# The two stores of the last product's halves issued from ScalarE's queue

## The chip, the cores and the metric

One core of a Trainium2 chip runs the whole kernel. The metric is the device time of one execution in microseconds (us); the kernel before takes 207.64 us, the median of three runs from 207.38 to 207.97. Its engines are TensorE (PE in the profile: matmuls, with PEld for weight loads), VectorE (DVE), ScalarE (ACT), GpSimd (POOL) and SyncE (SP), which computes nothing and issues transfers. Transfers can be issued from the instruction streams of SP, ACT and POOL; an issue is an instruction of that stream and waits there for what it needs.

## The reference

A decaying linear attention over 4 batches, 8 heads, 768 positions and 64 dimensions feeds a feed-forward layer with a leaky activation:

```python
for b in range(nb):                                    # blocks of 64 positions
    intra = (qb @ kb.T * Dmask) @ vb
    inter = (qb * lam_pow) @ kv_state
    out[block] = intra + inter
    kv_state = lam_block * kv_state + (kb * rev_pow).T @ vb
x = attn_out                                           # [3072, 512]
h = x @ w_in                                           # [3072, 2048]
g = max(h, 0) + alpha * min(h, 0)
return g @ w_out                                       # [3072, 512], float32
```

The change is in the way the last rows of `g @ w_out` are written out.

## The kernel before

The 3072 rows are worked through in six chunks of 512 (`c` from 0 to 5). A chunk holds 256 positions of two batches. For each, the attention part makes `xT` (512 features by 512 rows, fp16), `up` multiplies it by `w_in` and applies the activation, giving `g` in fp16, and a down projection multiplies `g` by `w_out`. The order of the instructions is written out by hand; every engine runs its stream in that order, and waits between engines are semaphores. Chunk `c`'s down projection runs among the up projection of chunk `c + 1`; the last chunk's comes after everything else, in `down2_last`, called in line 1105 as the last thing the kernel does.

The down projection of chunks 3 to 5 goes by seven products in place of eight: the rows of `g` are parted by even and odd positions, its features and the columns of `w_out` by halves, and sums and differences of these parts are multiplied. The products are numbered 1 to 7 and run in the order of `CHAIN` (line 640). Each product has eight matmuls of 128 rows by 256 columns for each batch `b`, in line 655. `evacuated` (line 673) then takes the result from PSUM: for products 1, 5, 6 and 4 ScalarE copies it into an output tile in SBUF (line 687), for 2, 3 and 7 VectorE adds it to such a tile (line 690). Products 2, 3, 4 and 7 each finish a quarter of the chunk's output, and `write` stores it.

In `down2_last` the two batches are taken one after the other, so each store has 128 rows of 256 floats, 128 KB. The last four steps are product 3 of batch 0, product 4 of batch 0, product 3 of batch 1, product 4 of batch 1. The very last one, `(i, b) == (4, 1)`, is cut into two halves of 128 columns (lines 714 to 720). Each half has a PSUM bank of its own ("s" and "acc"), eight matmuls, a VectorE add of 128x128 (line 719) to the tile `c21`, into which ScalarE has copied the sum so far (line 685), and a store of 64 KB by `write` (line 720).

All stores of the down projections are issued by SP, in line 589, 669 or 671. The nine of `down2_last` are those of line 671: seven of 128 KB and the two halves. After the last, SP waits until every transfer has landed (line 1131 in the profile, which is the end of the kernel), and a barrier of all engines closes it.

ScalarE issues one transfer in the kernel before, the load of `lam` in line 62.

Of the kernel before, what the change touches and what calls it, by code (L numbers as in the profile page):

```python
# [11 lines left out]
def kernel(  # L12
# [16 lines left out]
    nc = tc.nc  # L29
# [102 lines left out]
    def bank_of(bank, name, dtype=fp32):  # L132
        pool = h_ps_pool if bank == "h" else ps
        return pool.tile([128, CH], dtype, tag=bank, name=name)
# [25 lines left out]
    for half in range(2):  # L160
# [7 lines left out]
        out=drop, in0=rel_i, scalar1=0.0, scalar2=-1e30, op0=ALU.is_lt, op1=ALU.mult  # L168
# [458 lines left out]
    def g_sum(c, i, j, eng, b=None):  # L627

        a11, a12, a21, a22 = [part_of(c, j, half, e, b) for e in range(2) for half in range(2)]
        s1 = sums[3].rearrange("p f (b j) -> p f b j", b=2)[:, ds(2 * j, 2)]  # L630
        s1 = s1.rearrange("p i b j -> p i (b j)") if b is None else s1[:, :, b]
        out, in0, in1, op = {
            1: (s1, a21, a22, ALU.add),
            3: (a21, a11, a21, ALU.subtract),
            2: (a11, s1, a11, ALU.subtract),
            4: (a12, a12, a11, ALU.subtract),
        }[i]
        engine(eng).tensor_tensor(out=out, in0=in0, in1=in1, op=op)  # L638
# [3 lines left out]
    def product(c, i, b, t, fresh, last, cols, of=ds(0, 256)):  # L642

        for f in range(NF // 2):
            x = sums[3][:, f, ds(b * L, L)] if i == 5 else g_of(c, f + 8 * (i in (2, 3, 4)))[:, int(i in (4, 7)), b]
            w = {
                1: halves[0][0],
                2: halves[1][0],
                3: halves[1][1],
                4: sums[2],  # L650
                5: sums[0],
                6: sums[1],
                7: halves[0][1],
            }[i][:, f, of]
            nc.tensor.matmul(  # L655
                t[:, cols],
                lhsT=x,
                rhs=w,
                start=(fresh and f == 0),
                stop=(last and f == NF // 2 - 1),  # L660
                skip_group_check=True,
            )

    def write(c, e, half, o, b=None, of=ds(0, 256)):
        pb = c // 2
        to = out.rearrange("(x s) d -> x s d", x=B)[ds(2 * (c % 2), 2), ds(pb * W, W), ds(256 * half, 256)]
        to = to.rearrange("x (j e) d -> e j x d", e=2)[e]
        if b is None:
            nc.sync.dma_start(out=to, in_=o)
        else:  # L670
            nc.sync.dma_start(out=to[:, b, of], in_=o)

    def evacuated(c, i, t, b=None):

        X = O.setdefault((c, "out"), {})

        def tile_of(name):
            if name not in X:
                X[name] = o_pool.tile([128, 2, 256], fp32, tag="osb", name="o_sb")
            return X[name] if b is None else X[name][:, b]  # L680

        t = t.rearrange("p (x d) -> p x d", d=256) if b is None else t
        where = {2: ("c11", 0, 0), 3: ("c12", 0, 1), 4: ("c21", 1, 0), 7: ("c22", 1, 1)}
        if i is None:
            nc.scalar.activation(tile_of("c21"), t, AF.Copy)
        elif i in (1, 5, 6, 4):
            nc.scalar.activation(tile_of({1: "c11", 5: "c22", 6: "c12", 4: "c21"}[i]), t, AF.Copy)  # L687
        else:
            o = tile_of(where[i][0])
            nc.vector.tensor_tensor(out=o, in0=o, in1=t, op=ALU.add)  # L690
        if i in where:
            name, e, half = where[i]
            write(c, e, half, tile_of(name), b)
# [12 lines left out]
    def down2_last(c):  # L706

        order = [(i, side, b) for i, side in CHAIN[:5] for b in range(2)]
        order += [(3, 1, 0), (4, 0, 0), (3, 1, 1), (4, 0, 1)]
        for i, side, b in order:  # L710
            if i in (1, 2):
                O[c, side, b] = bank_of({(0, 0): "op", (1, 0): "tk"}.get((side, b), "h"), "o_ps")
            t = O[c, side, b]
            if (i, b) == (4, 1):
                for x, bank in enumerate(("s", "acc")):
                    p4 = ps.tile([128, 2, CH], fp32, tag=bank, name="p4")[:, 0]
                    product(c, i, b, p4, True, True, ds(0, 128), ds(128 * x, 128))
                    o = O[c, "out"]["c21"][:, b, ds(128 * x, 128)]
                    nc.vector.tensor_tensor(out=o, in0=o, in1=p4[:, 0:128], op=ALU.add)
                    write(c, 1, 0, o, b, ds(128 * x, 128))  # L720
                continue
            product(c, i, b, t, i in (1, 2, 5), i in (2, 3, 4), ds(0, 256))
            evacuated(c, i, t[:, 0:256], b)
            if (i, b) == (7, 1):
                evacuated(c, None, t[:, 0:256], b)
            if i == 1:
                for j in range(4):
                    g_sum(c, 2, j, "V", b)
            if i == 2 and b == 1:
                for j in range(4):  # L730
                    g_sum(c, 4, j, "V")
# [350 lines left out]
    for c, at in plan.items():  # L1082
        u = d = w = 0
        for x, what in enumerate(order[c]):
# [18 lines left out]
            if c == 4 and 9 <= x <= 12:  # L1103
                weight_sum(3, x - 9)
    down2_last(NC - 1)


# [28 lines left out]
```

## Time and profile before

| | |
|---|---|
| Median of three runs | 207.64 us (207.38 to 207.97) |
| The profiled execution | 207.89 us |
| Its span, first to last instruction | 206.1 us |
| Mean granted TensorE clock | 0.996 |
| PE busy | 200.1 us, 97% of the span |
| DVE busy | 159.1 us, 77% |
| ACT busy | 113.6 us, 55% |
| POOL busy | 110.3 us, 54% |
| Stores of line 671 | 9, the first issued at 193.9 us, the last at 203.2 us |
| Length of one such issue | shortest 332 ns, median 344 ns, longest 1178 ns |

The span leaves out what the run does around the program's first and last instruction, 1.8 us here. A row of the timeline has the start in us, the length in us, the engine, the line, the operation and the tiles; "SPq" and "ACTq" are the instruction streams of SP and ACT, where issues of transfers are listed and are not counted as busy. A row of the DMA view gives, for a stretch of time, the issues that began in it with their size and the time from issue to landing, that is until the transfer's completion was counted. "x2" at the end of a timeline row means that two neighbouring instructions were merged, with the gap between them in the length.

### The profile page before, as it was taken

What the parts mean: (1) busy time and instruction counts of PE and PEld (TensorE: products, weight loads), DVE (VectorE), ACT (ScalarE), POOL (GpSimd) and SP (SyncE); (2) the same over time, 40 slices, a digit from 0 to 9 for tenths busy, and PEclk for the clock granted to TensorE, in tenths of its full rate; (3) what the DMA queues carried; (4) which work ended last, traced back from release to release, by engine and by line L of the source; (5) the groups of instructions that cost most, each with busy time, mean ns of one, the idle gap of its engine ahead of it and who ended that gap; (6) DMA issues with size and microseconds to landing.
All of it is one profiled execution on the core that took longest, in us unless ns stands there. A gap on an engine that the chain in (4) does not pass through costs nothing.

```text
span 206.1 us, 5587 instructions
## 1 busy us (share of the span) xinstructions
PE 200.1 (97%) x2271; PEld 122.8 (60%) x2271; DVE 159.1 (77%) x289; ACT 113.6 (55%) x210; POOL 110.3 (54%) x132
## 2 busy tenths in 40 slices
PE   7999999999999999999999999999999999999991
PEld 6976445556445465555555455467667666667881
DVE  6978889568889647899998897959999466675921
ACT  7885778144776218656767466643543644444220
POOL 8999794043468893196356995562094040642000
PEclk9999999999999999999999999999999999999998
DMA  6999999997999998999969974441001201012222
GB/s 164 277 197 234 244 260 206 234 287 231 225 230 257 203 237 189 245 158 125 188 108 276 213 176 88 64 102 42 12 0 54 90 15 51 2 54 71 83 77 79
DMA packets 58206, 31.18 MB, mean 151 GB/s; under 512 B 27124, under 2 KB 55940, under 8 KB 58180
## 3 DMA queue, kind: packets, MB, share of 16 engines
q1 hardware_dynamic: 43028, 21.25, 42.5%
q0 software_dynamic: 15136, 9.57, 29.3%
q8 instruction: 18, 0.29, 0.6%
q14 instruction: 8, 0.07, 0.1%
q10 hardware_dynamic: 16, 0.00, 0.0%
HBM read 27.27 MB, written 6.29 MB: 163 GB/s over the span
## 4 chain that ended last, share of the span: by engine, by line
PE 92%; DVE 2%; ACT 2%; issue 1%; ACTq 0%; DVEq 0%
PE h_ps L545 39%; PE o_ps L573 21%; PE o_ps L655 16%; PE s L391 4%; PE acc L416 3%; PE unread L152 3%; PE acc L375 2%; PE tpx L341 2%; PE acc L436 1%; DVE g L638 1%; ACT L180 1%; ACT m L553 1%; ACT xT L250 1%; DVE sm L402 1%; PE p L655 0%
## 5 line engine op out<-in xcount | busy, mean ns | idle before, releaser
L545 PE MATMUL h_ps<-xT,w_in_sb 128*128 128x512 f16 (+1 forms) x392 | 91.9, 375 | 0.2 <-DVE g L560 0.2
L560 DVE SCALAR_TENSOR_TENSOR g<-m,oma,h_ps 128x512 f16<-128x512 f32 (+1 forms) x98 | 71.1, 734 | 24.9 <-ACT m L553 21.7
L553 ACT ACTIVATE m<-h_ps 128x512 f32<-128x512 f32 (+1 forms) x98 | 57.3, 588 | 46.3 <-PE h_ps L545 40.3
L545 PEld LDWEIGHTS <-w_in_sb 128*128 128x128 f16 x392 | 37.6, 98 | 37.4 <-issue 0.4
L573 PE MATMUL o_ps<-w_out_sb,g 128*128 128x512 f16 x192 | 46.8, 380 | 0.0
L402 DVE TENSOR_TENSOR sm<-s,dmask 128x1024 f16<-128x1024 f32 x24 | 29.2, 1219 | 11.7 <-PE s L391 11.7
L655 PEld LDWEIGHTS <-g 128*128 128x128 f16 x296 | 28.2, 98 | 8.2
L638 POOL TENSOR_TENSOR s<-g 128x512 f16<-128x512 f16 x11 | 13.0, 1179 | 32.8 <-PE o_ps L655 16.7
L573 PEld LDWEIGHTS <-g 128*128 128x128 f16 x192 | 17.7, 98 | 19.4 <-DVE g L560 0.2
L250 ACT ACTIVATE xT<-acc 128x512 f16<-128x512 f32 x24 | 14.3, 597 | 24.2 <-PE acc L436 22.2
L355 POOL TENSOR_TENSOR qdT<-qkT,qdecay 128x512 f16<-128x512 f16 (+1 forms) x19 | 20.5, 1082 | 7.6 <-DMA qkT<-qk 4.5
L655 PE MATMUL o_ps<-w_out_sb,g 128*128 128x256 f16 x192 | 24.1, 273 | 0.0
L291 POOL TENSOR_TENSOR kdec<-kraw,kdecay 128x512 f16<-128x512 f32 x18 | 20.0, 1116 | 6.1 <-DMA kraw<-in_k_dram 6.0
L254 POOL CAST qk<-qraw 128x512 f16<-128x512 f32 x12 | 7.6, 637 | 16.7 <-DMA qraw<-in_q_dram 15.9
L465 DVE SCALAR_TENSOR_TENSOR R<-R,rdecay,acc 128x128 f16<-128x128 f16 x54 | 15.5, 340 | 0.0
L278 POOL DMA_DIRECT2D v<-in_v_dram x19 | 14.9, 789 | 0.4 <-issue 0.4
L638 POOL TENSOR_TENSOR g<-g 128x512 f16<-128x512 f16 x11 | 13.3, 1207 | 0.9
L687 ACT ACTIVATE o_sb<-o_ps 128x512 f32<-128x512 f32 (+1 forms) x15 | 7.5, 497 | 7.6 <-PE o_ps L655 7.6
L655 PE MATMUL o_ps<-w_sum,g 128*128 128x256 f16 x88 | 11.3, 273 | 0.0
L391 PE MATMUL s<-qkT 64*64 64x128 f16 x384 | 10.1, 221 | 0.0
L416 PE MATMUL acc<-sm,v 64*64 64x128 f16 x384 | 9.8, 218 | 0.0
L690 DVE TENSOR_TENSOR o_sb<-o_sb,o_ps 128x512 f32<-128x512 f32 (+1 forms) x12 | 6.5, 549 | 4.2 <-PE o_ps L655 2.2
(84 smaller groups left out, 194.2 us busy)
## 6 DMA issues: line engine op xcount, KB each, us to landing
out_dram<-o_sb SPq DMA_DIRECT2D x20, 256.0 KB, 3.0
kraw<-in_k_dram SPq DMA_DIRECT2D x7, 512.0 KB, 5.3
qraw<-in_q_dram SPq DMA_DIRECT2D x6, 512.0 KB, 5.5
v<-in_v_dram POOLq DMA_DIRECT2D x19, 128.0 KB, 5.1
w_in_sb<-in_moe_w_in_dram POOLq DMA_DIRECT2D x4, 512.0 KB, 8.5
w_out_sb<-in_moe_w_out_dram POOLq DMA_DIRECT2D x4, 512.0 KB, 10.5
qraw<-in_q_dram POOLq DMA_DIRECT2D x6, 256.0 KB, 7.1
qraw<-in_q_dram SPq DMA_DIRECT2D x6, 256.0 KB, 4.8
```

Of the source, the lines that this page charges most:

```text
L250: nc.scalar.activation(out, in_, AF.Copy)
L291: engine(eng).tensor_tensor(out=kdec, in0=kr, in1=kdecay[:, ds(4 * hh, 4), :].rearrange("p h e -> p e h").unsqueeze(3).to_broadcast([128, ...
L355: engine(eng).tensor_tensor(out=qdT[:, :, :, p], in0=(t["qps"] if eng == "P" else t["qkT"][:, 0])[:, :, :, p], in1=qdecay[:, hh, :, :, p], ...
L391: nc.tensor.matmul(t["s"][ds(a * 64, 64), hl, hp, 1 - e, :].rearrange("p (e j) -> p e j", e=2), lhsT=t["qkT"][p, 1, e, hp, ds(a * 64, 64)] ...
L402: nc.vector.tensor_tensor(out=t["sm"].rearrange("p a h x j -> p (a h) x j"), in0=t["s"].rearrange("p a h x j -> p (a h) x j"), in1=mask_of ...
L416: nc.tensor.matmul(ot[a][ds(hl * 64, 64), hp, :], lhsT=t["v16"][p, 2 * hp + hl, e, :], rhs=t["sm"][p, hl, hp, 1 - e, :], start=(2 * pb + a ...
L545: nc.tensor.matmul(h_ps[:, 0:n] if bi is None else h_ps[:, 0:n].rearrange("p (e j) -> p e j", e=2), lhsT=w_in_sb[:, gi, ts(f, 128)], rhs=x ...
L553: nc.scalar.activation(m[:, 0:n], h_ps[:, 0:n], AF.Relu, scale=-1.0)
L560: nc.vector.scalar_tensor_tensor(out=g, in0=mv, scalar=oma[:, f : f + 1], in1=hv, op0=ALU.mult, op1=ALU.add)
L573: nc.tensor.matmul(o_ps, lhsT=lhs(c, f, t), rhs=w_out_sb[:, f, :], start=(f == 0), stop=(f == NF - 1),)
L638: engine(eng).tensor_tensor(out=out, in0=in0, in1=in1, op=op)
L655: nc.tensor.matmul(t[:, cols], lhsT=x, rhs=w, start=(fresh and f == 0), stop=(last and f == NF // 2 - 1), skip_group_check=True,)
```

## The change

`write` gets a parameter for the engine whose stream issues the store, with SP as its default, and the call for the two halves of the last product passes ScalarE. All other calls stay on SP.

```diff
-    def write(c, e, half, o, b=None, of=ds(0, 256)):
+    def write(c, e, half, o, b=None, of=ds(0, 256), queue=nc.sync):
...
         if b is None:
             nc.sync.dma_start(out=to, in_=o)
         else:
-            nc.sync.dma_start(out=to[:, b, of], in_=o)
+            queue.dma_start(out=to[:, b, of], in_=o)
...
                     nc.vector.tensor_tensor(out=o, in0=o, in1=p4[:, 0:128], op=ALU.add)
-                    write(c, 1, 0, o, b, ds(128 * x, 128))
+                    write(c, 1, 0, o, b, ds(128 * x, 128), nc.scalar)
```

Two of the nine stores of line 671 are thereby issued from ScalarE's stream, with the same tiles, sizes and places in the output as before.

## The prediction

> **What bounds the kernel now.** I read the page's engine table and its chain of waits first, then the timeline of the last six microseconds, then the DMA view of narrow windows there, and last what SyncE (SP) waits for at the end.
>
> ```profile
> PE 200.1 (97%) x2271; PEld 122.8 (60%) x2271; DVE 159.1 (77%) x289; ACT 113.6 (55%) x210; POOL 110.3 (54%) x132
> PE 92%; DVE 2%; ACT 2%; issue 1%; ACTq 0%; DVEq 0%
> 201.00 0.91 PE p L655 x16
> 201.93 0.29 DVE o_sb L719
> ```
>
> The first two lines are the engines' busy time and the chain's shares, the other two the end of the chain in order of time (start, length, what). Up to 201.9 us TensorE is the bound, and the change touches none of it. But the chain stops at the last VectorE add, at 201.93 + 0.29 = 202.22, and the span is 206.1. What lies in the 3.9 us between is stores, and the change is there and nowhere else.
>
> ```profile
> 200.16 0.38 ACT L687 ACTIVATE o_sb<-o_ps 128x256 f32<-128x256 f32 x1 [0.84 <-PE o_ps L655]
> 201.03 0.42 DVE L690 TENSOR_TENSOR o_sb<-o_sb,o_ps 128x256 f32<-128x256 f32 x1 [1.32 <-PE o_ps L655]
> 201.54 0.68 DVE L719 TENSOR_TENSOR o_sb<-o_sb,p 128x128 f32<-128x128 f32 x2
> 199.74 0.33 SPq L671 DMA_DIRECT2D out_dram<-o_sb  x1
> 200.57 0.33 SPq L671 DMA_DIRECT2D out_dram<-o_sb  x1
> 201.48 1.18 SPq L671 DMA_DIRECT2D out_dram<-o_sb  x1
> 202.75 0.38 SPq L671 DMA_DIRECT2D out_dram<-o_sb  x1
> 203.23 0.41 SPq L671 DMA_DIRECT2D out_dram<-o_sb  x1
> ```
>
> These are timeline rows: start, length, engine. The last five stores start at 199.74, 200.57, 201.48, 202.75 and 203.23; call the last three A, B and C. B and C are the two halves that the change moves. A is the store of the product before, and stays on SP. A's data are ready at 201.03 + 0.42 = 201.45 and it starts 0.03 later, so SP is on time there. But issuing A takes 1.18 us, where the two stores of the same size ahead of it took 0.33. B's data are ready when the first of the two adds at L719 ends; the pair runs from 201.54 to 202.22 and the second starts at 201.93, so the first, as long as the second, ends at 201.83. SP gets to B at 202.75, 0.92 late, and to C at 203.23, 1.01 late. That lateness is what the change can win.
>
> ```profile
> DMA packets 28, 0.04 MB, mean 440 GB/s; under 512 B 0, under 2 KB 27, under 8 KB 27
> q8 instruction: 1, 0.02, 100.9%
> 202.27:202.66 0.39, 0.00 (x0) 0.00 (x0) 0.00 (x0) 0.00 (x0) 0.00 (x0) 1.00 0.08 11
> q8 instruction: 1, 0.02, 57.4%
> 155.56 0.38 SPq L669 DMA_DIRECT2D out_dram<-o_sb  x1
> ```
>
> Why A takes so long: the first two rows are the DMA view of 200.6 to 200.7. One packet in it is not a store's but an instruction fetch, 16 KB in one packet and so on one DMA engine of 16. Its share, 100.9% of 16 engines' 0.1 us, makes 1.61 us, so that engine is taken until about 202.3. The third row is a stretch of the windows view (its last two columns are DMA share and GB/s): from 202.27 to 202.66 only 0.08 of the 16 engines is busy, one engine or little more, which is the late one making up its part of earlier stores. A's issue ends at 202.66, 0.4 after the fetch: an ordinary issue, begun when the late engine came free. The last two rows are a fetch between 155.5 and 155.6 with a single store beside it, which took its usual 0.38. So a fetch alone doesn't hold an issue; it held A, when that engine already owed parts of earlier stores.
>
> ```profile
> out_dram<-o_sb SPq DMA_DIRECT2D x1, 128.0 KB, 2.7
> out_dram<-o_sb SPq DMA_DIRECT2D x1, 64.0 KB, 1.7
> SPq L1131 <- DMA out_dram<-o_sb: 0.5, 2, 0.3
> SPq L1131 <- DMA out_dram<-o_sb: 0.4, 1, 0.4
> L1131 SPq EVENT_SEMAPHORE  x11: 17/28/28, 203.7 to 206.1; - x11
> L1131 SPq DRAIN  x3: 7/7/13, 205.3 to 205.6; - x3
> ```
>
> Landings: A lands 2.7 after its start, at 201.48 + 2.7 = 204.2; B at 202.75 + 1.7 = 204.45; C at 203.23 + 1.7 = 204.94. The waits are SP's at the end of the kernel, in 204 to 204.25 and in 204.55 to 205: it waits for these landings in their order and last for C. From C's landing to the span's end are 206.1 - 204.94 = 1.16 us of closing waits and barriers, which the change leaves alone.
>
> **The change, part by part.** Removed: two issues of 0.38 and 0.41 on SP, the last two that it has. Added: the same two on ScalarE (ACT), each behind the wait for VectorE's add that it had on SP. No byte, add or matmul changes.
>
> Where they land on ACT: its last operation ends at 200.16 + 0.38 = 200.54. Behind the moved issues there is only the closing drain, so nobody is held by a wait there. ACT's idleness is the cover for the 0.8 us of issuing; an ACT busy past 202.7 would take the gain away.
>
> They are moved past one item of SP's queue, A. If ACT can issue while A is held on SP: B starts at 201.83 + 0.03 = 201.86 and takes 0.38, to 202.24. C's data are there at 202.22, and the gap between B and C on SP was 203.23 - 202.75 - 0.38 = 0.10, so C starts at 202.34 and lands at 202.34 + 1.7 = 204.04. That is before A's landing at 204.2. What is late next is A, on SP. So the end moves from 204.94 to 204.2, 0.74 us, and no further.
>
> Two things come off. SP looks at the landings in order and has, after A's, two more waits to pass, where now it has none of these after C. Between C's landing at 204.94 and its drain at 205.3 it passes some five waits, about 0.07 each, an estimate from the rows above; two make 0.14, hence 0.6. And B's and C's packets now fall into the time of A's.
>
> ```profile
> 203.15:203.64 0.49, 0.00 (x0) 0.00 (x0) 0.00 (x0) 0.00 (x0) 0.00 (x0) 1.00 0.79 272
> 204.10:204.50 0.40, 0.00 (x0) 0.00 (x0) 0.00 (x0) 0.00 (x0) 0.00 (x0) 0.98 0.55 164
> ```
>
> A's packets fill 203.15 to 203.64 at 0.79 of the engines; C's take 0.55 x 0.40 = 0.22 us of all 16. If C starts moving 0.47 after its issue ends, as A does (202.66 to 203.15), it is under way from 203.2 and at worst puts A's end off by 0.22; at best it fits beside A (0.21 of the engines is free). I take 0.06, nearer to nothing, since B is through by then. The sum: 0.74 - 0.14 - 0.06 = 0.54 us.
>
> What an issue of this size costs on ACT no row shows. The nearest are SP's stores (0.33 to 0.41, and 1.18 when held) and ACT's single issue in the kernel, a load of a few bytes:
>
> ```profile
> 0.73 0.59 ACTq L62 DMA_DIRECT2D lam_sb<-in_lam_dram  x1
> 0.74 0.46 SPq L89 DMA_DIRECT2D kraw<-in_k_dram  x1
> ```
>
> At 0.59 each, C's issue would end at 201.86 + 0.59 + 0.10 + 0.59 = 203.14, 0.50 before its end now (203.64), and land 0.50 earlier: a gain of 0.50 less the same 0.06. I take SP's price, which belongs to the same transfer. So the mechanism is worth 0.38 (0.6 less the full 0.22) to 0.6.
>
> Against the profiled execution's 207.89 (206.1 of span and 1.8 around it) the sum is 207.35. That execution is 0.25 above the median of the three runs, 207.64; the part that changes is the same, so the forecast is 207.64 - 0.54 = 207.10, a ratio of 0.9974.
>
> **The rivals.** *First: one issue at a time.* If SP's held issue also holds ACT's, B can't start before 202.66. It then takes 0.38, C starts at 203.14 and lands at 204.84: 0.10 won, from the gap between A and B alone; 207.54. For it: at the kernel's start SP and ACT issue together, and ACT's, far smaller, took 0.59, just past the end of SP's 0.46. Against it: both are recorded as under way in the same 0.46 us, and SP's, with far more packets, is the shorter of the two.
>
> The Trainium skill, Perfetto Trace Analysis, section "DMA Instruction — HWDGE (DVE, Sync)", has this rule: the descriptor generator is shared between two sequencers, and one issue locks it until its descriptors are all made. By that rule the outcome is this rival's 207.54; the pair of rows at the start fits it and doesn't prove it.
>
> *Second: the hold is not in every run.* The three times spread from 207.38 to 207.97, more than the forecast. Without the fetch in the way A's issue would take 0.33 and end at 201.81, B would start on time and C 0.1 after its data at most. The change would be worth nothing to 0.1: 207.6. Against it: TensorE runs the same instructions at the same times in each execution, so the fetch should fall on the same stores.
>
> *Third, slower: the halves go ahead of A.* When the late engine comes free, B and C are waiting for it beside A. If both are served before A, SP's issue ends by two issues later, at 202.66 + 0.38 + 0.41 = 203.45. A's landing follows its issue's end by 2.7 - 1.18 = 1.52, so A lands at 204.97, with the two waits at 205.11: 0.17 slower. At ACT's 0.59 for each the end is 203.84, and with the waits 205.50: 0.56 slower, 208.2. It decides once A's issue ends past 203.28, 0.62 later than now. I take the middle, 0.35: 208.0. For it: A is held by exactly that engine, and B and C need it too. Against it: A has asked 0.38 us before B.
>
> **How the numbers follow.** Forecast 0.55, one issue at a time 0.20, no hold 0.10, halves ahead 0.15. No change means within 0.3%, 0.62 us, about what a measurement of this kernel can tell. The forecast's 0.54 lies close under that bound, and the three runs alone spread over 0.28%, so I give a bit more than half of its chance to faster: 0.33, and 0.05 from the two cases beside it by scatter. Slower takes half of the third rival, 0.08, and 0.04 of scatter. That is 0.38, 0.50, 0.12. The likeliest case's own range is 206.9 to 207.3, from its 0.38 to 0.6 and 0.15 of scatter. With the other cases the range reaches up to 207.95, just short of the third rival's middle, and down to 206.75 for scatter below.
>
> **What would show it.** Right: two store issues on ACT at about 201.86 and 202.34 of 0.4 each, A's issue on SP still near 1.2, the last closing wait on A, and a span of 205.6. First rival: B's issue on ACT long, about 0.8 to 1.2, ending after 203.0. Second: A's issue near 0.33 in the new profile. Third: A's issue over 1.5 and A the last to land, after 204.9. The forecast is wrong above all if ACT's issues don't run beside a held SP, or if A moves.

## The result, and the profile after

| | Kernel before | Changed kernel |
|---|---|---|
| Median, 20 runs each, taken together | 207.70 us | 207.24 us |
| Ratio, 95% interval | | 0.9977 (0.9968 to 0.9985) |
| Profiled execution, its span | 207.89 us, 206.1 us | 207.43 us, 205.7 us |

The change wins 0.46 us of 207.7, clear of the scatter of the runs. Forecast was 0.54, a ratio of 0.9974. Both lie under the 0.3% up to which the prediction speaks of no change, its likeliest outcome at 0.50.

The page's engine table, the end of the chain of waits (start, length) and the timeline of the changed kernel's last three issues (start, length, engine) answer to the rows quoted before the result.

```profile
PE 200.0 (97%) x2271; PEld 122.7 (60%) x2271; DVE 159.7 (78%) x289; ACT 113.6 (55%) x210; POOL 110.0 (53%) x132
```

```profile
201.01 0.91 PE p L655 x16
201.92 0.02 issue
201.94 0.29 DVE o_sb L719
```

```profile
201.50 0.33 SPq L671 DMA_DIRECT2D out_dram<-o_sb  x1
...
201.87 0.37 ACTq L671 DMA_DIRECT2D out_dram<-o_sb  x1
202.28 0.46 ACTq L671 DMA_DIRECT2D out_dram<-o_sb  x1
```

TensorE's work is as it was, and the last add ends at 201.94 + 0.29 = 202.23, where it ended at 202.22 before. So the gain lies in the tail after it: 205.65 - 202.23 = 3.42 us against 3.90. From here on "the tail" is this stretch, from the end of the last add at line 719 to the end of the span, A is the third-last store, and B and C are the two halves. B and C are issued on ScalarE within 0.06 us of where the prediction put them (201.86 and 202.34) and cost about what it took for them. Two things are not as it said. A, which stays on SP, is issued in 0.33 us, not 1.2. And C is still the last to land, as the DMA view of these three issues (time to landing in the last column) and SP's waits at the end show, both of the changed kernel. The third fence is its DMA view of 201.2 to 201.3 and of 203.6 to 204.1, the fourth its windows view, whose last two columns are DMA share and GB/s:

```profile
out_dram<-o_sb SPq DMA_DIRECT2D x1, 128.0 KB, 2.6
...
out_dram<-o_sb ACTq DMA_DIRECT2D x1, 64.0 KB, 2.4
...
out_dram<-o_sb ACTq DMA_DIRECT2D x1, 64.0 KB, 2.2
```

```profile
SPq L1131 <- DMA out_dram<-o_sb: 2.2, 2, 1.9
```

```profile
q8 instruction: 1, 0.02, 65.2%
...
q10 hardware_dynamic: 18, 0.01, 5.6%
```

```profile
203.60:204.10 0.50, 0.00 (x0) 0.00 (x0) 0.00 (x0) 0.00 (x0) 0.00 (x0) 1.00 0.06 18
```

A lands at 201.50 + 2.6 = 204.1, B at 204.3, C at 202.28 + 2.2 = 204.5. SP, which has nothing left to issue after 201.83, now waits 2.2 us for landings in all. Before, a half landed 1.7 after its start; here it takes 2.2 to 2.4 though nothing held its issue. The fetch is there again: 65.2% of 16 engines' 0.1 us is 1.04 us, in the trace from 201.24 to 202.28. The last two rows say who is late: from 203.60 to 204.10 the DMA share is 0.06, one engine of 16, and 18 of its 20 packets are of ScalarE's queue (q10). The two halves have 288 packets in all, so 18 are a sixteenth of them. It is one engine's part of B and C that comes last.

### The profile page after: what moved, and what is told of

It reads as the page before. It is cut to its first block, busy times and chain, and to the rows that moved or that the text cites. A ratio compares the mean times of both kernels' runs of the same rounds, so it can differ in the third digit from the quotient of the medians.

```text
span 205.7 us, 5585 instructions
## 1 busy us (share of the span) xinstructions
PE 200.0 (97%) x2271; PEld 122.7 (60%) x2271; DVE 159.7 (78%) x289; ACT 113.6 (55%) x210; POOL 110.0 (53%) x132
## 4 chain that ended last, share of the span: by engine, by line
PE 92%; DVE 2%; ACT 2%; issue 1%; ACTq 0%; DVEq 0%
PE h_ps L545 40%; PE o_ps L573 21%; PE o_ps L655 16%; PE s L391 4%; PE acc L416 3%; PE unread L152 2%; PE acc L375 2%; PE tpx L341 2%; PE acc L436 1%; DVE g L638 1%; ACT L180 1%; ACT m L553 1%; ACT xT L250 1%; DVE sm L402 1%; PE p L655 0%
## 5 line engine op out<-in xcount | busy, mean ns | idle before, releaser
L355 POOL TENSOR_TENSOR qdT<-qkT,qdecay 128x512 f16<-128x512 f16 (+1 forms) x19 | 21.1, 1116 | 8.5 <-DMA qkT<-qk 5.3
L291 POOL TENSOR_TENSOR kdec<-kraw,kdecay 128x512 f16<-128x512 f32 x18 | 19.2, 1069 | 6.5 <-DVE g L560 5.4
```

The costliest lines, as they stand in the source:

```text
L291: engine(eng).tensor_tensor(out=kdec, in0=kr, in1=kdecay[:, ds(4 * hh, 4), :].rearrange("p h e -> p e h").unsqueeze(3).to_broadcast([128, ...
L355: engine(eng).tensor_tensor(out=qdT[:, :, :, p], in0=(t["qps"] if eng == "P" else t["qkT"][:, 0])[:, :, :, p], in1=qdecay[:, hh, :, :, p], ...
```

## The experiments

The kernels were compared with the kernel before on the same chip. Where a time has an interval, the medians are of 5 to 12 runs of the kernel, and of 20 for the change itself. Tails, starts and landings are read from each kernel's profiled execution. The last column but one is the time from the end of the fetch's packet (its start and length in the trace) to the last landing.

| Kernel | A's issue, us | C's start after the last add | Tail | Last landing after the fetch | Median, ratio (95%) |
|---|---|---|---|---|---|
| before | 1.18 (SP) | 1.02 | 3.90 | 2.65 | 207.70 |
| before, again | 0.84 (SP) | 0.68 | 3.56 | 2.66 | 207.32, one run |
| changed | 0.33 (SP) | 0.06 | 3.42 | 2.20 | 0.9977 (0.9968 to 0.9985) |
| changed, again | 1.05 (SP) | 0.05 | 3.27 | 2.15 | 207.25, one run |
| only first half on ScalarE | 1.18 (SP) | 0.54 | 3.42 | 2.17 | 207.09, 0.9975 (0.9966 to 0.9984) |
| only second half on ScalarE | 1.12 (SP) | 0.09 | 3.78 | 2.54 | 207.68, 1.0002 (0.9986 to 1.0018) |
| only A on ScalarE | 0.37 (ScalarE) | 0.36 | 3.41 | 2.39 | 207.50, 0.9985 (0.9967 to 1.0002) |
| no late fetch, stores as before | 0.33 (SP) | 0.17 | 3.05 | - | 207.06, 0.9961 (0.9946 to 0.9976) |
| no late fetch, both halves on ScalarE | 0.33 (SP) | 0.05 | 3.00 | - | 207.03, 0.9960 (0.9944 to 0.9975) |
| no late fetch, second half on ScalarE | 0.33 (SP) | 0.09 | 2.97 | - | 206.99, 0.9962 (0.9949 to 0.9976) |

"No late fetch" in the table is the late split described below; four runs with another warm-up, which moved the fetch too, stand in the second part.

**Both kernels once more.** No edit; the question was whether A's hold is in every execution.

> The kernel before, unchanged, to see whether the hold of the third-last store is in every execution. If the prediction's account holds, its issue takes 1.0 to 1.3 us again, an instruction fetch of 16 KB ends near 202.3 us, and from the end of the last VectorE add to the end of the span it is 3.9 us (206.12 - 202.21 = 3.90 in the profile shown). If the hold comes and goes (second rival), that issue takes 0.33 and the tail is near 3.4.

> The changed kernel, unchanged, to see whether the third-last store on SP is again not held (0.33 in its first profile) and what ends last. If the absence of the hold is chance, the issue can be 1.2 here, with ScalarE's two issues still short (0.37 and 0.46); if the hold depends on the halves' being on SP's queue, it is 0.33 again. The tail from the last add to the span's end was 205.65 - 202.23 = 3.42 and should be 3.4 to 3.5 either way.

Timeline rows of the kernel before, taken again (A, C and the last add), and then of the changed kernel, taken again (A, B and C):

```profile
201.16 0.84 SPq L671 DMA_DIRECT2D out_dram<-o_sb  x1
202.56 0.40 SPq L671 DMA_DIRECT2D out_dram<-o_sb  x1
201.60 0.29 DVE L719 TENSOR_TENSOR o_sb<-o_sb,p 128x128 f32<-128x128 f32 x1
```

```profile
201.47 1.05 SPq L671 DMA_DIRECT2D out_dram<-o_sb  x1
201.84 0.37 ACTq L671 DMA_DIRECT2D out_dram<-o_sb  x1
202.25 0.43 ACTq L671 DMA_DIRECT2D out_dram<-o_sb  x1
```

The hold varies: 1.18 and 0.84 in two executions of the kernel before, 0.33 and 1.05 in two of the changed one, with the fetch in the tail each time. It doesn't hang on where B and C are issued. The tails, 3.56 and 3.27, were not the expected 3.9 and 3.4 to 3.5.

What stays the same is measured from the fetch. In all five executions in which A is held on SP, A's issue ends 0.37 to 0.38 us after the fetch's packet. The last landing follows that packet by 2.65 and 2.66 us in the kernel before and by 2.20 and 2.15 in the changed one, held or not. So from the fetch's end the change is worth 0.45 to 0.51 us, near the 0.46 of the timed runs. The tails differ more because the fetch ends anywhere from 0.28 us before the last add's end to 0.08 after it.

The second fence also answers the first rival: while A is held on SP, from 201.47 to 202.52, ScalarE issues B in 0.37. The hold is of one queue, not of both.

**The fetch taken out of the tail by another warm-up.** The 56 warm-up matmuls of 128 columns at line 756 became 28 of 256 columns, or 100 of 72, with SP's stores and with the changed queue. TensorE's stream is then 56 instructions shorter or 88 longer, and its fetches fall elsewhere.

```diff
-    tick(56, "tk")
+    [nc.tensor.matmul(t[:, 0:256].rearrange("p (a j) -> p a j", a=2), lhsT=ident, rhs=ident.unsqueeze(1).to_broadcast([128, 2, 128]), start=True, stop=True) for t in [bank_of("tk", "unread")] for _ in range(28)]
```

```diff
-    tick(56, "tk")
+    [nc.tensor.matmul(t[:, 0:72], lhsT=ident, rhs=ident[:, 0:72], start=True, stop=True) for t in [bank_of("tk", "unread")] for _ in range(100)]
```

> The kernel before, with 56 of the warm-up matmuls at the kernel's start done as 28 of twice the width, so that TensorE's stream is 56 instructions shorter and its last instruction fetch falls behind the end. If the fetch's engine is what delays the tail: no fetch after 190 us, no late share, the third-last store issued in 0.33, the halves at 201.9 and 202.37, the last landing near 204.1, a tail of 3.0 to 3.1 us, 0.8 us under the kernel before and faster than the changed kernel, about 206.8. If the tail is instead set by SP's serial issuing, the tail stays at 3.4 or above.

> The changed kernel with the same 28 wide warm-up matmuls. If the change only goes around the delay that the fetch causes, this run and the one with SP's stores differ by 0.1 us or less (C issued at 202.28 in place of 202.37): about 206.75. If two queues are better in themselves, the changed queue still wins 0.4 to 0.5 us over the other run, about 206.35.

> The kernel before, with the 56 warm-up matmuls of 128 columns done as 100 of 72 columns, so that TensorE's stream is 88 instructions longer and its last instruction fetch comes some 44 matmuls earlier, between 195.5 and 197 us instead of 200.6 to 202.3, when no store is under way. If the fetch in the tail is the cause: the third-last store issued in 0.33, no late landing, a tail of 3.05 us from the last add to the span's end (3.90 and 3.56 in the two profiles of the kernel before), and, if the warm-up takes no longer, about 207.0 us, faster than the changed kernel. If the tail is set by SP's serial issuing alone: a tail of 3.4 or more.

> The changed kernel with the same 100 narrow warm-up matmuls. If the change only goes around the delay of the fetch: a tail of 3.0 and a time within 0.1 us of the run with SP's stores, about 206.95. If two queues win by themselves: 0.4 us less than that run.

The tails came out as the fetch account says: 3.05 and 3.04 with SP's stores, 3.01 and 3.00 with the changed queue, and A issued in 0.33 in all four. The last fetch that is left is over by 196.1 in the wide and by 199.3 in the narrow kernel (with SP's stores), before the last five stores begin. Without the fetch the change is worth 0.04 to 0.05 us of tail. The totals missed: 209.76 (ratio 1.0119, 1.0090 to 1.0148) and 209.80 (1.0107, 1.0088 to 1.0127) for the wide warm-up, 208.92 (1.0083, 1.0052 to 1.0115) and 210.59 (1.0134, 1.0106 to 1.0162) for the narrow one. Something at the start got worse. Rows of the windows view, 10 to 20 us, of the kernel before, of the wide and of the narrow warm-up with SP's stores (PE busy is the second number, the clock the third from the end):

```profile
10.00:20.00 10.00, 9.59 (x235) 6.71 (x235) 8.18 (x16) 7.74 (x18) 9.98 (x14) 1.00 1.36 205
```

```profile
10.00:20.00 10.00, 8.59 (x220) 6.27 (x219) 7.46 (x14) 6.01 (x14) 9.98 (x14) 0.83 1.35 200
```

```profile
10.00:20.00 10.00, 8.15 (x239) 6.06 (x240) 7.96 (x16) 6.74 (x15) 9.76 (x14) 1.00 1.36 202
```

TensorE stands idle 1.0 to 1.4 us more there, in one case at a lower granted clock too, which was still 0.82 from 20 to 30 us. The clock also parts the runs of the narrow warm-up: with SP's stores four had a mean of 0.998 to 1.000 and took 208.2 to 208.9 us, three had 0.989 to 0.992 and took 210.1 to 210.6; with the changed queue five of six were at the lower clock. Whether the loss comes from the warm-up itself or from the fetches' new places among the first loads stays open; for the totals these runs say nothing of the change.

**The fetch taken out late.** Ten of the sixteen up projections of chunk 4 run as twice as many matmuls of half the columns, 80 instructions more, so that the start stays as it is.

```diff
-        for gi in range(NHP):
-            x = XT[c][:, gi]
+        for gi, k in [(y, z) for y in range(NHP) for z in range(2 if c == 4 and f % 8 < 5 else 1)]:
+            x, s = XT[c][:, gi], ts(k, 256) if c == 4 and f % 8 < 5 else ds(0, n)
...
-                h_ps[:, 0:n] if bi is None else h_ps[:, 0:n].rearrange("p (e j) -> p e j", e=2),
+                h_ps[:, s] if bi is None else h_ps[:, 0:n].rearrange("p (e j) -> p e j", e=2),
...
-                rhs=x.rearrange("p e b j -> p (e b j)") if bi is None else x[:, :, bi, :],
-                start=(gi == 0),
+                rhs=x.rearrange("p e b j -> p (e b j)")[:, s] if bi is None else x[:, :, bi, :],
+                start=(gi == 0 and k == 0), skip_group_check=c == 4,
```

> The kernel before, with ten of the sixteen up projections of chunk 4 (near 150 to 185 us) done in matmuls of 256 columns instead of 512, the same columns in all: 80 more TensorE instructions, all late, so that the last fetch comes 4 us earlier, between 196 and 198 us, and the start of the kernel is as it was. If the fetch in the tail is the cause and the fetches' places at the start are what slowed the runs with other warm-ups: a tail of 3.05 us, and 207.0 us (207.7 less 3.73 - 3.05 = 0.7, the mean of the two tails of the kernel before), without any store moved. If TensorE pays for the narrower matmuls: up to 207.7.

> The same ten up projections split, with the changed queue. If the change only goes around the fetch's delay: a tail of 3.0 and the same time as with SP's stores within 0.1 us, about 206.95, which is under both kernels. If two queues win by themselves: 0.4 us under that run.

Rows of the run with SP's stores: A, B and C in the timeline, then the DMA view with the fetch (of 196.5 to 196.6) and their landings.

```profile
201.75 0.33 SPq L671 DMA_DIRECT2D out_dram<-o_sb  x1
202.18 0.38 SPq L671 DMA_DIRECT2D out_dram<-o_sb  x1
202.65 0.41 SPq L671 DMA_DIRECT2D out_dram<-o_sb  x1
```

```profile
q8 instruction: 1, 0.02, 79.6%
...
out_dram<-o_sb SPq DMA_DIRECT2D x1, 128.0 KB, 1.9
out_dram<-o_sb SPq DMA_DIRECT2D x1, 64.0 KB, 1.7
out_dram<-o_sb SPq DMA_DIRECT2D x1, 64.0 KB, 1.7
```

The fetch is over by 197.9 (196.6 + 1.27), A lands in 1.9, where it took 2.4 to 2.8 in the seven profiles with the fetch in the tail, and the last store 1.7 after its start. With all stores on SP this wins 0.70 us, more than the change does; with the changed queue on top it is 207.03 against 207.06, the same. So once the fetch is away the change is worth 0.05 us of tail and nothing that these medians can tell. Both are faster than the kernel before; next to the changed kernel (0.9977) their intervals overlap, and by the ratios they lie 0.16% under it.

**One half alone.** The call for the halves passes ScalarE for one of them only:

```diff
-                    write(c, 1, 0, o, b, ds(128 * x, 128), nc.scalar)
+                    write(c, 1, 0, o, b, ds(128 * x, 128), (nc.scalar, nc.sync)[x])
```

and `(nc.sync, nc.scalar)[x]` for the other run.

> Only the first half's store on ScalarE, the second stays on SP right behind the third-last. With the hold the second half then starts when that issue ends, near 202.7, 0.5 earlier than before and 0.4 later than with both moved: a tail of 3.4 to 3.5 and 207.25 to 207.4. If the gain is the issue time taken off SP, half of it: 207.45.

> Only the second half's store on ScalarE, the first stays on SP behind the third-last. If the gain is that the last store no longer queues behind the other two, the second half starts 0.06 after the last add and the first lands 0.1 to 0.2 later than it did with both moved: a tail of 3.3 to 3.5 and nearly the whole gain, 207.25 to 207.4. If the gain is the issue time taken off SP, half of it: 207.45.

With the first half alone the whole gain is there (207.09). With the second alone there is none, which was not expected. Timeline rows of A, B and C and the landing of C on SP, of the run with the first half on ScalarE; then the timeline rows of A, C and B and the landings of C and B, of the run with the second:

```profile
201.16 1.18 SPq L671 DMA_DIRECT2D out_dram<-o_sb  x1
201.53 0.38 ACTq L671 DMA_DIRECT2D out_dram<-o_sb  x1
202.43 0.38 SPq L671 DMA_DIRECT2D out_dram<-o_sb  x1
```

```profile
out_dram<-o_sb SPq DMA_DIRECT2D x1, 64.0 KB, 1.7
```

```profile
201.71 1.12 SPq L671 DMA_DIRECT2D out_dram<-o_sb  x1
202.53 0.38 ACTq L671 DMA_DIRECT2D out_dram<-o_sb  x1
202.92 0.38 SPq L671 DMA_DIRECT2D out_dram<-o_sb  x1
```

```profile
out_dram<-o_sb ACTq DMA_DIRECT2D x1, 64.0 KB, 2.3
out_dram<-o_sb SPq DMA_DIRECT2D x1, 64.0 KB, 2.1
```

In both the last issue on SP waits for A's. In the first it is C alone, 0.54 after the last add, and it lands in 1.7. In the second B starts 0.48 after the last add and takes 2.1. By then C has been issued on ScalarE across the end of A's hold, and the three issues end within half a microsecond (A 202.83, C 202.91, B 203.30). Whether they get in each other's way there isn't shown. The last packets of C and B start 1.65 and 1.86 us after the last add, about when the changed kernel's do (1.84), but the landings are counted 0.74 and 0.70 behind them, in the changed kernel 0.42 to 0.45. Nor is it enough that an issue on ScalarE crosses the end of A's hold: in the second profile of the changed kernel C's does (202.25 to 202.69, the hold's end at 202.52), with a tail of 3.27. A run with the same placing and no late fetch asks whether the placing is to blame by itself:

> Only the second half's store on ScalarE, with the ten up projections split so that the fetch lies before the tail. If the run with this store alone on ScalarE lost its gain because its issue and the first half's ran into the end of the held one, then without a hold both are on time: the first half issued on SP 0.3 before the last add's end, the second on ScalarE 0.06 to 0.1 after it, a tail of 3.0 to 3.1 and 207.0 to 207.1. If a store of the second half on ScalarE is late by itself, a tail of 3.3 or more.

It gave 206.99, ratio 0.9962 (0.9949 to 0.9976), and a tail of 2.97. C on ScalarE alone does no harm in itself; it takes the fetch in the tail to spoil it, and how it does so stays open.

**A alone.** The store of product 3 of the second batch goes to ScalarE, the halves stay on SP:

```diff
-            write(c, e, half, tile_of(name), b)
+            write(c, e, half, tile_of(name), b, queue=nc.scalar if (c, i, b) == (NC - 1, 3, 1) else nc.sync)
...
-                    write(c, 1, 0, o, b, ds(128 * x, 128), nc.scalar)
+                    write(c, 1, 0, o, b, ds(128 * x, 128))
```

> Only the third-last store, the one that is held, issued on ScalarE; both halves stay on SP, which then has two stores ahead of them as it had ahead of the third-last. If a queue is held when its third store comes while the fetch's engine is behind, the third-last is issued in about 0.4 on ScalarE, the first half is held on SP until the fetch ends (0.6 to 0.8 long) and the second follows: the second half starts 0.45 to 0.6 after the last add in place of 1.0, a tail of 3.4 to 3.5 and 207.25. If the hold goes with the store or with the generator of the issues and not with the queue, the third-last takes 0.8 to 1.2 on ScalarE too.

Timeline rows of this run, A, B, C:

```profile
201.38 0.37 ACTq L671 DMA_DIRECT2D out_dram<-o_sb  x1
201.74 0.63 SPq L671 DMA_DIRECT2D out_dram<-o_sb  x1
202.46 0.44 SPq L671 DMA_DIRECT2D out_dram<-o_sb  x1
```

A on ScalarE isn't held, and B is in its place (0.63 where B takes 0.38). That is what a hold of SP's queue at its third store would do, with the late engine owing parts of the first two. The tail is 3.41 as expected, the time 207.50 and not 207.25; its interval touches 1, so how much of the gain this keeps is open. From the fetch's end its last landing, 2.39, lies between the two kernels.

## Why the prediction was right, and where it was not

**The bound and the place of the change: right.** TensorE's work and the last add stayed, and the tail after the add went from 3.90 to 3.42.

**The fetch as the cause: right, and shown.** A held issue ends 0.37 to 0.38 after the fetch, in every execution with a hold of A on SP. With the fetch moved ahead of the tail, A is issued in 0.33, every landing is back at 1.7 to 1.9, and the tail is 3.0 with either queue, in seven runs.

**ScalarE's cost: right.** 0.37 and 0.46 for the two issues, where 0.38 and 0.41 were taken, at 201.87 and 202.28. Nothing on ScalarE was held up.

**The first rival: out.** ScalarE issues in 0.37 while SP stands held. The Trainium skill, Perfetto Trace Analysis, section "DMA Instruction — HWDGE (DVE, Sync)", has the generator locked by one issue until its descriptors are made; for the time of the hold these traces show no such lock. Whether one acts at the end of the hold, where the second half alone on ScalarE lost the gain, they don't tell.

**The second rival: half right as an observation.** The hold does change from run to run, 0.33 to 1.18 in the six profiles with the fetch in the tail and A on SP. But the fetch was in the tail in all six, and in the changed kernel's two profiles the hold costs nothing: the unheld execution has a tail of 3.42, no shorter than the held one, 3.27. What the change is worth against a kernel before that has the fetch and no hold isn't shown, as no such execution was profiled.

**The third rival: not seen.** A landed at 204.13 in both profiles with the halves on ScalarE, no later than before (204.21). In the second one B did get ahead of A and landed at 203.95, but A lost nothing by it.

**The step that was mis-sized: what is late next.** The prediction let C land 1.7 after its start, at 204.04, and made A's landing at 204.2 the end, with 0.14 for two more closing waits and 0.06 for shared engines. Measured, C took 2.2 and landed at 204.5, last (2.04 and 204.3 in the second profile, last again). The 1.7 held only for parts of the store on engines that were up to date. The engine that had the fetch still owed parts of the two stores ahead of A, of A, and then of B and C, and did them one after the other until 204.1: its last packets of the five start at 202.99, 203.33, 203.68, 203.87 and 204.07. The prediction saw that engine as the reason for the hold on SP and left it out of C's own landing. So the end moved 204.94 - 204.48 = 0.46 us in this pair of profiles. The two deductions, 0.20 together, stood by chance close to the missing term of 0.28 (0.74 - 0.46): with C last, no further waits came behind the last landing, and A was not put off.

**A's issue staying at 1.2: not a fixed number.** The prediction's profile had the longer hold of the two of that kernel, and the changed kernel's first profile had none. The forecast came out nevertheless, because with B and C on ScalarE only A stands behind the hold, and A is not the last to land. By single pairs of tails the change wins from 0.14 to 0.63; measured from the fetch's end it is 0.45 to 0.51.

## What to carry to other kernels

Where the last stores of a kernel land later than stores of the same size before them, look in the DMA view for an instruction fetch beside them: here one engine of 16 held up for 1 to 1.6 us delayed its part of every store, whichever queue issued it. A second queue gets around a held queue, not around a late engine; moving the fetch (here by 80 instructions more in the same TensorE time) removes both. Here it was enough to take the store in the middle off the queue (207.09), while moving the last one alone won nothing (207.68).

## What the runs showed of the hardware

- A fetch of 16 KB for TensorE's instructions is one packet on one DMA engine and took 1.0 to 1.6 us in these tails. A lone store issued with it took 0.38 as ever; the third one out on SP took up to 1.18. Why one execution in six had no hold at all stays open. Its fetch starts 0.6 us later in the trace than in the kernel before (201.2 and 200.7), but the late engine owed no less: when A was issued, 135 of the 144 packets of the store two ahead of it had gone, 15 engines' part, in all seven profiles with the fetch in the tail, and all 144 in those with the late split. So what the engine owes does not make a hold by itself.
- Splitting ten groups of 128x512 matmuls in halves by columns cost no time that these runs can tell (0.9961 with a tail that is 0.7 shorter).
- Warm-up matmuls of about the same total columns but another count cost 1.3 to 2.9 us in the whole kernel. TensorE was idle longer from 10 to 20 us, and some runs had a lower granted clock. The cause was not settled.
